# Block-sparse attention and a gated feed-forward layer on one core: scores issued a position ahead of their exponentials, and the gathered values shared between GpSimd and SyncE

## The chip, the cores and the metric

The kernel runs on one core of a Trainium2 chip. The time is that of one execution on the device, in microseconds. Its engines are TensorE (PE, with its weight loads as PEld), VectorE (DVE), ScalarE (ACT), GpSimd (POOL) and SyncE (SP), which here only starts transfers. Each runs its own instruction stream in order; they wait for one another by semaphores.

## The reference

```python
B, H, S, D = q.shape                    # 4, 8, 768, 64; blocks of 32, so 24 blocks
mask = np.abs(blk_i - blk_j) <= 1       # a window of three blocks,
mask |= (blk_i == 0) | (blk_j == 0) | (blk_i == 23) | (blk_j == 23)   # first and last block global,
for qb in range(24):
    for kb in sampled_blocks[qb]:       # and three sampled blocks for each query block
        mask[qb*32:(qb+1)*32, kb*32:(kb+1)*32] = True
attn = softmax(where(mask, q @ k.T / sqrt(D), -1e9))
x = (attn @ v).transpose(0, 2, 1, 3).reshape(3072, 512)
xn = x / sqrt(mean(x*x) + 1e-6) * rms_g
out = (silu(xn @ w_gate) * (xn @ w_val)) @ w_out    # 512 -> 1536 -> 512
```

The sampled blocks are input data: which keys and values a query block needs is known only when the kernel runs.

## The kernel before

Batch 0 is computed densely, in groups of 256 queries; this takes about the first 72 us, and the other batches' keys and queries are loaded and turned beside it. Batches 1 to 3 are computed sparsely, in 18 **chunks** of four query blocks, six chunks to a batch. Five are ordinary (four consecutive blocks); the sixth, the wide one, holds blocks 0, 23, 1 and 22. Blocks 0 and 23 attend to every key, so a wide chunk has eight score bursts instead of four.

For a query block, keys and values lie in 128 rows: slots for the first and the last block, the three window blocks, the three sampled ones, each stored as 16 pairs of rows. Keys are collected in `kg` by copies: the window by DVE (`gather_k`, L471), the sampled blocks by ACT and GpSimd (`sampled_k`, L485), queries by DVE (`gather_q`, L500). Values are collected in `vg` from a table in device memory (`vtab`, L446) by one indirect gather of GpSimd for each query block (`gather_v`, L512), four for an ordinary chunk, two for a wide one, 66 in all. `vg` has two buffers in use; a third is laid over what the dense phase needs.

**Sequence of a chunk.** The loop over the chunks (L1078) runs 19 times, and each turn has ten positions. Jobs are registered for a position by `do(n, f)`. In turn i:

- position 0: the values of chunk i−1 in two halves (`values`, L644, 64 or more small matmuls each), TensorE turns of some chunks, and GpSimd's key copies for the next chunk
- positions 1 and 2: `normalise` of the two halves on DVE (reciprocal L669, multiplication L670)
- positions 1 to 4 (wide: 1 to 8): `scores(i, part)`: eight 64-column matmuls into one PSUM bank (L620), and directly behind them their exponential on ACT (L628), into `ex`, which has three buffers
- position 2: the gathers for the next chunk's values
- positions 3, 4 and 6: DVE's copies of queries and keys for the next chunk; ACT's key copies are spread up to position 9
- position 4: squares on ACT (L677); position 5: `rms_power` on GpSimd (L681, L682); position 7: `x_scaled` on DVE (L698), with a DMA transpose on SyncE (L700) into `xg`, or for four chunks later by TensorE (L707).

Behind every position, `position()` (L798) takes pieces of the feed-forward layer from a list, at a rate that is worked out when a group of chunks enters (groups of 2, 3, 4, 4, 3 and 2 chunks; a group enters at position 4 of the second turn after its last chunk). A **piece** is a gate (L737, then `th` on ACT at L741), a value (L748; `u` at L752 and `hps` at L756 on DVE) or a down projection (L766, then `yo` on ACT at L771 and a store by SyncE at L717 or L726). So TensorE's stream is attention with feed-forward pieces between, in an order that the program fixes; after the last chunk (254 us) only the last group's feed-forward is left.

**PSUM.** Every burst, half of the values, gate, value and down piece takes the next of eight banks in a ring (`bank()`, L103). The next user of a bank waits until the reader of the old content is done.

Of the kernel before, what the change touches and what calls it, by code (L numbers as in the profile page):

```python
# [18 lines left out]
def kernel(  # L19
# [12 lines left out]
    nc = tc.nc  # L32
# [70 lines left out]
    def bank(shape, dtype, name):  # L103
        space, tag = ring[turn_of[0] % len(ring)]
        turn_of[0] += 1
        return space.tile(shape, dtype, name=name, tag=tag)
# [27 lines left out]
    def load_v(b, pr):  # L134
        t = vraw[(b, pr)] = ld.tile([P, 2, NC, D], FP32, name="vraw", tag="vraw", bufs=4)
        if b:
            nc.vector.memset(t[0:1, 0, 0, 0:1], 0.0)
        (nc.sync if b else nc.gpsimd).dma_start(
            out=t, in_=v[b, 2 * pr:2 * pr + 2].rearrange("e (p c) d -> p e c d", p=P))
# [213 lines left out]
    qb_i = const.tile([NS, NB], I32, name="qb_i")  # L353
    vidx = const.tile([P, NB], I32, name="vidx")
    kofs = const.tile([1, NB * NRND], I32, name="kofs")
    qb = const.tile([NS, NB], FP32, name="qb")
    rs = const.tile([NS, NB, NRND], FP32, name="rs")
    pp_i = const.tile([NS, 1], I32, name="pp_i")
# [25 lines left out]
    def index_steps():  # L384
# [24 lines left out]
        for r, lo, hi in ((1, 0, 2 * HB), (0, 0, HB), (2, 2 * HB, 3 * HB)):  # L409
            yield lambda r=r, lo=lo, hi=hi: nc.vector.tensor_scalar(  # L410
                out=vidx[lo:hi], in0=tmp[lo:hi, :, r], scalar1=float(HB), scalar2=pp[lo:hi],
                op0=ALU.mult, op1=ALU.add)


    kat = {}
    ET = mybir.EngineType
# [4 lines left out]
    def address(c, r, n=1):  # L421
        eng = ET.Activation if by_act(c, r) else ET.Pool
        _, vals = nc.values_load_multi_w_load_instructions(
            kofs[0:1, r * NB + c:r * NB + c + n], engines=[eng], min_val=0, max_val=NT - HB,
            skip_runtime_bounds_check_because="a sampled block is one of the sequence's")
        for m, x in enumerate(vals):
            kat[(c + m, r)] = x

    by_need = [(x, r) for i in range(PB) for x in chunks[i][1] if x not in (0, NB - 1)
               for r in range(NRND) if by_act(x, r)]  # L430
# [74 lines left out]
                            in_=spaced(rows[:, :, qbs[lo] * HB:(qbs[lo] + 1) * HB],  # L505
                                       (qbs[lo + 1] - qbs[lo]) * HB, hi - lo, HB))

    def gather_v(i, js=range(QB)):
        b, qbs = chunks[i]
        for j in js:  # L510
            if qbs[j] not in (0, NB - 1):
                nc.gpsimd.indirect_dma_start(  # L512
                    vgs[i % 2][:, j, :], None, vtab[b][:],
                    bass.IndirectOffsetOnAxis(ap=vidx[:, qbs[j]:qbs[j] + 1], axis=0))


    def ex_tile():
# [86 lines left out]

    exs = {}

    def bursts(i):
        return 8 if chunks[i][1][0] == 0 else 4

    def scores(i, part):  # L610
        b, qbs = chunks[i]
        wide = qbs[0] == 0
        heads = H // bursts(i)
        st = bank([P, 512], FP32, "st")
        at = 0
        for h in range(part * heads, (part + 1) * heads):
            of = [(KT[b % 2][:, h, cc::HC], j) for cc in range(HC) for j in range(2)] if wide else []
            of += [(kgs[i % 2][:, h, j, :], j) for j in range(2 if wide else 0, QB)]
            for lhsT, j in of:
                nc.tensor.matmul(  # L620
                    out=st[:, at:at + UN], lhsT=lhsT,
                    rhs=Qd[i % 2][:, h, :, :, j * HB:(j + 1) * HB].rearrange("p a w s -> p (a w) s"),
                    start=True, stop=True)
                at += UN
        if part % 4 == 0:
            exs[(i, part // 4)] = work.tile([P, 4 * 512], BF16, name="ex", tag="ex", bufs=3)
        ex = exs[(i, part // 4)][:, part % 4 * 512:(part % 4 + 1) * 512]
        nc.scalar.activation(  # L628
            out=ex.rearrange("p (u s w) -> p u s w", s=HB, w=2),
            in_=st.rearrange("p (u w s) -> p u s w", s=HB, w=2), func=AF.Exp, scale=SCALE)  # L630

    ops, stages, ssqs, rstds = {}, {}, {}, {}

    def values(i, g):
        b, qbs = chunks[i]
        wide = qbs[0] == 0
        op = bank([P, 512], FP32, "op")
        ops.setdefault(i, []).append(op)
        vg = vgs[i % 2].rearrange("p j (w h x) -> p j w h x", w=2, h=H)
        per = H // bursts(i)  # L640

        def mm(h, j, lhsT, rhs, n, of):
            at = (h % 4) * VW
            nc.tensor.matmul(out=op[j * BLK:(j + 1) * BLK, at:at + VW], lhsT=lhsT, rhs=rhs,  # L644
                             start=(n == 0), stop=(n == of - 1))

        for h in range(4 * g, 4 * g + 4):
            part = h // per
            ex = exs[(i, part // 4)][:, part % 4 * 512:(part % 4 + 1) * 512].rearrange(
                "p (h u w s) -> p h u w s", h=per, w=2, s=BLK)[:, h % per]  # L650
            if not wide:
                for w in range(2):
                    for j in range(QB):
                        mm(h, j, ex[:, j, w, :], vg[:, j, w, h, :], w, 2)
                continue
            for n in range(NC):
                cc, w = divmod(n, 2)
                for j in range(2):
                    mm(h, j, ex[:, 2 * cc + j, w, :], Vs[b % 2][:, 2 * cc + w, h, :], n, NC)
                if n < 2:  # L660
                    for j in range(2, QB):
                        mm(h, j, ex[:, 4 + j, n, :], vg[:, j, n, h, :], n, 2)

    def normalise(i, g):
        if g == 0:
# [184 lines left out]
    def side_work(gi, h):  # L850
# [23 lines left out]
        if gi == 2:  # L874
            if h == 0:
                nc.vector.memset(Vs[1][:, :, :, D:VW], 1.0)
                for b in range(1, B):
                    zero_rows(b)
            if h == 1:
                load_kq(1, 3)  # L880
            if h in (2, 3):
                cast_v(1, 2 * h - 4, pool)
                cast_v(1, 2 * h - 3, pool)
            if h == 3:
                table(1)
                nc.vector.tensor_scalar(out=gain, in0=gain, scalar1=float(DM) ** 0.5,
                                        scalar2=None, op0=ALU.mult)
                nc.vector.memset(eps, DM * 1e-6)
            if h in (3, 4):
                load_kq(2, h - 3)  # L890
            if h > 3:
                load_v(2, h - 4)
            if h == 5:
                gather_v(0)
                for x in sampled_k(0, "pool"):
                    x()
                first_keys.extend(sampled_k(0, "act"))
                first_copies.extend(gather_k(0, dve))
            if h == 7:
                gather_v(1, (0, 1))  # L900
                load_kq(2, 2)

    first_keys, first_copies = [], []
# [174 lines left out]
    for i in range(NCH + 1):  # L1078
        jobs = {}

        def do(n, f):
            jobs.setdefault(n, []).append(f)
# [4 lines left out]
        if i == 0:  # L1087
# [5 lines left out]
            do(6, lambda: enter_dense(cur, distance(0, 6)))  # L1093
            do(4, lambda: nc.vector.memset(Qd[1], 0.0))
            do(3, lambda: load_kq(2, 3))
            do(7, lambda: gather_v(1, (2, 3)))
        else:
            do(0, lambda: values(i - 1, 0))
            do(0, lambda: values(i - 1, 1))
# [7 lines left out]
            if i - 2 in by_pe:  # L1107
                do(0, lambda: x_turned(i - 2))
        if i < NCH:
            n = bursts(i)  # L1110
            for part in range(n):
                do(1 + part, lambda part=part: scores(i, part))
        if b + 1 < B and s <= NP:
            if s < NP:
                do(9 if s == 0 else 0, lambda: cast_v(b + 1, s, act))
# [7 lines left out]
        if nx is not None:  # L1123
# [17 lines left out]
            for m, x in enumerate(kact):  # L1141
                do(at + (m + 1) * (NPOS - 1 - at) // len(kact), x)

            if nx > 1:
                do(2, lambda: gather_v(nx))
        for m in range(min(6, len(by_need)) if i < 2 else 0):
            do(m, next_address)

# [48 lines left out]
```

## The time and the profile before

| | |
|---|---|
| median of three runs | 290.3 us (289.85 to 290.57) |
| the profiled execution | 290.28 us, of it span 288.5 us |
| GpSimd: gathers L512 | 66, mean 992 ns, 65.5 us |
| ACT: exponentials L628 | 84, mean 600 ns, 50.4 us |
| TensorE: gate, value and down pieces L737, L748, L766 | 80.2, 80.0 and 69.1 us |
| DVE: `u` L752 and `hps` L756 | 54.5 and 55.1 us |
| DMA traffic | 47.44 MB, of it 32.60 MB on GpSimd's queue and 14.18 MB on SyncE's |
| start of the values calls, us | 81.5, 90.25, 100.2, 108.8, 115.8, 126.4, 136.1, 145.0, 153.5, 162.3, 172.0, 183.2, 194.3, 202.5, 213.7, 226.7, 239.0, 253.9 |

Times in the profile are microseconds from the start of the span. "Idle before" an instruction is the time its engine stood still ahead of it, and an arrow names what ended it. A row of a stage lists for each engine its busy time in that stretch. A matmul's record covers its way through the array, so records of matmuls that follow one another overlap; what a row of them costs is read from start to start.

### The profile page before, as it was taken

The page shows a single profiled execution, that of the slowest core. Times are in us where ns is not written, and L with a number is a line of the kernel's source. Part 1 is how long each engine was busy: PE and PEld are TensorE (multiplying, and loading weights), DVE is VectorE, ACT ScalarE, POOL GpSimd, SP SyncE. Part 2 cuts the span into 40 slices and gives each one's busy share as a digit, 9 for nine tenths or more (in the row PEclk, how much of TensorE's full clock was granted, in tenths as well). Part 3 has the DMA queues.
Part 4 walks back from the last instruction along what each step waited for, and adds up shares of the span by engine and source line. Part 5 has one row for each costly group of instructions (what it writes and reads, how often), then busy time and mean ns, then how long its engine had stood idle before and what let it go on. Part 6 is the DMA issues. An engine that isn't in the chain of part 4 may idle for free.

```text
span 288.5 us, 9875 instructions
## 1 busy us (share of the span) xinstructions
PE 273.9 (95%) x3840; PEld 185.3 (64%) x3871; DVE 216.7 (75%) x596; ACT 198.2 (69%) x467; POOL 146.7 (51%) x244
## 2 busy tenths in 40 slices
PE   8798999898999899799999999999999999999995
PEld 6586896687668678666665555545545556664783
DVE  7888889678979959966999578796499951784580
ACT  4896786588589789759989878577746484533331
POOL 8857244558487585787887627627723330101000
PEclk9999999999999999999999999999999999999999
DMA  7999999999885479898995845426932252000102
GB/s 133 287 214 201 206 207 268 290 229 315 168 232 125 142 205 287 173 222 259 250 170 154 280 122 154 101 73 186 204 115 77 59 168 77 36 2 36 75 1 73
DMA packets 37426, 47.44 MB, mean 164 GB/s; under 512 B 11184, under 2 KB 29380, under 8 KB 37380
## 3 DMA queue, kind: packets, MB, share of 16 engines
q0 software_dynamic: 21184, 32.60, 51.1%
q1 hardware_dynamic: 16132, 14.18, 17.2%
q8 instruction: 30, 0.49, 0.7%
q14 instruction: 16, 0.13, 0.1%
q10 hardware_dynamic: 64, 0.03, 0.0%
HBM read 46.45 MB, written 8.83 MB: 192 GB/s over the span
## 4 chain that ended last, share of the span: by engine, by line
PE 64%; DVE 16%; DMA 11%; issue 3%; POOL 3%; ACT 2%; DVEq 0%; ACTq 0%; POOLq 0%
PE yp L766 19%; PE gp L737 16%; PE vp L748 15%; PE st L620 5%; DMA gain<-in_moe_rms_g_dram 5%; DVE u L752 4%; DVE hps L756 4%; DMA qbf<-in_q_dram 4%; PE op L644 4%; DMA vraw<-in_v_dram 3%; PE tqk L455 2%; PE st L527 2%; DVE stage L670 1%; DVE xs L698 1%; PE op L536 1%
## 5 line engine op out<-in xcount | busy, mean ns | idle before, releaser
L512 POOL DMA_INDIRECT vg<-vtab,vidx x66 | 65.5, 992 | 45.2 <-PE op L644 27.1
L737 PE MATMUL gp<-xg,wg 128*128 128x256 bf16 (+2 forms) x426 | 80.2, 307 | 2.2 <-DVE stage L670 0.9
L748 PE MATMUL vp<-xg,wv 128*128 128x256 bf16 (+2 forms) x428 | 80.0, 307 | 1.4 <-DVE u L752 0.6
L741 ACT ACTIVATE th<-gp 128x256 bf16<-128x256 f32 (+2 forms) x108 | 49.8, 463 | 37.6 <-PE gp L737 34.4
L752 DVE SCALAR_TENSOR_TENSOR u<-th,gp 128x256 bf16<-128x256 bf16 (+2 forms) x108 | 54.5, 504 | 22.1 <-ACT th L741 21.5
L766 PE MATMUL yp<-wo,hps 128*128 128x512 bf16 (+1 forms) x282 | 69.1, 370 | 1.6 <-issue 0.3
L756 DVE TENSOR_TENSOR hps<-u,vp 128x256 bf16<-128x256 bf16 (+2 forms) x108 | 55.1, 510 | 11.6 <-PE vp L748 0.5
L628 ACT ACTIVATE ex<-st 128x512 bf16<-128x512 f32 x84 | 50.4, 600 | 13.8 <-PE st L620 12.6
L737 PEld LDWEIGHTS <-wg 128*128 128x128 bf16 x432 | 39.7, 98 | 20.0 <-issue 2.0
L748 PEld LDWEIGHTS <-wv 128*128 128x128 bf16 x432 | 39.5, 98 | 18.6 <-issue 1.5
L766 PEld LDWEIGHTS <-hps 128*128 128x128 bf16 x300 | 26.1, 98 | 20.8 <-DMA wo<-in_moe_w_out_dram 0.3
L530 ACT ACTIVATE ex<-st 128x768 bf16<-128x768 f32 x42 | 33.3, 813 | 5.8 <-PE st L527 5.6
L771 ACT ACTIVATE yo<-yp 128x512 f32<-128x512 f32 (+1 forms) x25 | 14.6, 582 | 19.7 <-PE yp L766 19.5
L681 POOL TENSOR_TENSOR ssq<-ssq,eps 128x1 f32<-128x1 f32 x18 | 4.3, 241 | 39.6 <-ACT junk L677 38.1
L527 PE MATMUL st<-wide_q,wide_k 88*128 88x256 bf16 x144 | 22.9, 272 | 1.5 <-DVE wide_q L345 1.1
L644 PEld LDWEIGHTS <-ex 128*32 128x32 bf16 x1344 | 13.6, 95 | 7.8 <-issue 7.8
L670 DVE TENSOR_TENSOR stage<-op,rz 128x256 bf16<-128x256 f32 x36 | 15.3, 425 | 1.2
L644 PE MATMUL op<-vg,ex 128*32 128x66 bf16 x1056 | 15.2, 195 | 1.0 <-DVE u L752 1.0
L527 PEld LDWEIGHTS <-wide_k 88*128 88x128 bf16 x144 | 13.0, 97 | 5.0 <-DVE wide_q L345 2.0
L620 PEld LDWEIGHTS <-kg 128*128 128x128 bf16 x272 | 12.7, 98 | 5.2 <-issue 0.3
L620 PEld LDWEIGHTS <-wide_q 128*128 128x128 bf16 x256 | 12.5, 98 | 5.3 <-issue 0.2
L620 PE MATMUL st<-wide_q 128*128 128x64 bf16 x256 | 15.1, 193 | 0.1
(147 smaller groups left out, 379.6 us busy)
## 6 DMA issues: line engine op xcount, KB each, us to landing
out_dram<-yo SPq DMA_DIRECT2D x20, 256.0 KB
vraw<-in_v_dram SPq DMA_DIRECT2D x12, 384.0 KB
kbf<-in_k_dram POOLq DMA_DIRECT2D x15, 192.0 KB, 5.7
vtab<-Vs POOLq DMA_DIRECT2D x3, 792.0 KB, 6.2
qbf<-in_q_dram POOLq DMA_DIRECT2D x12, 192.0 KB, 8.4
vraw<-in_v_dram POOLq DMA_DIRECT2D x4, 384.0 KB, 6.4
wg<-in_moe_w_gate_dram POOLq DMA_DIRECT2D x4, 384.0 KB, 10.6
wv<-in_moe_w_val_dram POOLq DMA_DIRECT2D x4, 384.0 KB
```

Of the source, the lines that this page charges most:

```text
L512: nc.gpsimd.indirect_dma_start(vgs[i % 2][:, j, :], None, vtab[b][:], bass.IndirectOffsetOnAxis(ap=vidx[:, qbs[j]:qbs[j] + 1], axis=0))
L527: nc.tensor.matmul(out=at[:, e], lhsT=KT0[0:KR, h, jt * P:(jt + 1) * P], rhs=QT0[0:KR, h, c0 * P:(c0 + 2) * P], start=True, stop=True)
L530: nc.scalar.activation(out=ex[:, 3 * part:3 * (part + 1), :], in_=at[:, 0:3], func=AF.Exp, scale=SCALE)
L620: nc.tensor.matmul(out=st[:, at:at + UN], lhsT=lhsT, rhs=Qd[i % 2][:, h, :, :, j * HB:(j + 1) * HB].rearrange("p a w s -> p (a w) s"), sta ...
L628: nc.scalar.activation(out=ex.rearrange("p (u s w) -> p u s w", s=HB, w=2), in_=st.rearrange("p (u w s) -> p u s w", s=HB, w=2), func=AF.E ...
L644: nc.tensor.matmul(out=op[j * BLK:(j + 1) * BLK, at:at + VW], lhsT=lhsT, rhs=rhs, start=(n == 0), stop=(n == of - 1))
L737: nc.tensor.matmul(out=gp[:, 0:tg], lhsT=wg[:, c, f * P:(f + 1) * P], rhs=xg[:, c, 0:tg], start=(c == 0), stop=(c == KD - 1))
L741: nc.scalar.activation(out=th[:, 0:tg], in_=gp[:, 0:tg], func=AF.Tanh, scale=0.5)
L748: nc.tensor.matmul(out=vp[:, 0:tg], lhsT=wv[:, c, f * P:(f + 1) * P], rhs=xg[:, c, 0:tg], start=(c == 0), stop=(c == KD - 1))
L752: nc.vector.scalar_tensor_tensor(out=u[:, 0:tg], in0=th[:, 0:tg], scalar=1.0, in1=gp[:, 0:tg], op0=ALU.add, op1=ALU.mult)
L756: nc.vector.tensor_tensor(out=hps[f][:, 0:tg], in0=u[:, 0:tg], in1=vp[:, 0:tg], op=ALU.mult)
L766: nc.tensor.matmul(out=yp, lhsT=hps[f][:, tt * P:(tt + 1) * P], rhs=wo[:, f, lo:hi], start=(f == 0), stop=(f == NF - 1))
```

## The change

- `scores` is split: the matmuls of part p of an ordinary chunk are issued at position p, the exponential stays at position 1 + p, as a function of its own (`exponentials`). For a wide chunk the eight bursts stand at positions 0, 1, 1, 2, 3, 3, 4, 5 and the exponentials at 1 to 8. In turn 0 all of them are a position later.
- In a wide chunk the matmuls for blocks 0 and 23, which have the same keys, are merged into one of 128 columns.
- Values: for an ordinary chunk blocks 0 and 1 are still gathered by GpSimd, and blocks 2 and 3 come by SyncE's transfers (`fetch_v`): one for the windows of both blocks, one for each sampled block, whose row is a register's value, and broadcasts of the first and last block, which are left out where the buffer still has them. Of a wide chunk, GpSimd gathers one block and SyncE fetches one.
- GpSimd's gathers are now for the chunk after the next, two positions behind an exponential (`behind` copies one element of `ex`, so the queue of GpSimd waits for it). SyncE's transfers, also for the chunk after the next, are at position 8.
- Three buffers of `vg` are used in turn.
- The three indices of a block are packed into one number by DVE and loaded into SyncE's registers in the dense phase (`table_blocks`).

```diff
+    def table_row(c, r):
+        at = nc.s_assert_within((vat[c] >> (5 * r)) & 31, 0, NB, ...)
+        return at * HB
...
-    def gather_v(i, js=range(QB)):
+    def gather_v(i, js):
...
-                    vgs[i % 2][:, j, :], None, vtab[b][:],
+                    vgs[i % 3][:, j, :], None, vtab[b][:],
...
+    def by_pool(i):
+        return (2,) if wide(i) else (0, 1)
+
+    def fetch_v(i):
+        b, qbs = chunks[i]
+        vg, t = vgs[i % 3], vtab[b]
+        j0 = by_pool(i)[-1] + 1
+        n = QB - j0
+        for to, at, none in ((F0, 0, 1), (L0, NT - HB, NB - 2)):
+            if none in qbs[j0:]:
+                at = NT
+            elif i % PB > 2:
+                continue
+            src = t[at:at + HB, :]
+            nc.sync.dma_start(
+                out=vg[to:to + HB, j0:QB, :], in_=src.unsqueeze(1).to_broadcast([HB, n, 2 * HV]))
+        w = t[(qbs[j0] - 1) * HB:(qbs[j0] + 2) * HB, :]
+        step = (qbs[j0 + 1] - qbs[j0]) * HB if n > 1 else 0
+        nc.sync.dma_start(
+            out=vg[W0:W0 + 3 * HB, j0:QB, :],
+            in_=_dc.replace(w.unsqueeze(1), ap=[w.ap[0], [step * 2 * HV, n], w.ap[1]]))
+        for j in range(j0, QB):
+            for r in range(NRND):
+                nc.sync.dma_start(out=vg[R0 + r * HB:R0 + (r + 1) * HB, j, :],
+                                  in_=vtab[b][bass.ds(table_row(qbs[j], r), HB), :])
+
+    def behind(i, part):
+        nc.gpsimd.tensor_copy(out=gate, in_=exs[(i, part // 4)][0:1, part % 4 * 512:part % 4 * 512 + 1])
...
+            if wide(i):
+                for cc in range(HC):
+                    nc.tensor.matmul(
+                        out=st[:, 2 * cc * UN:2 * (cc + 1) * UN], lhsT=KT[b % 2][:, h, cc::HC],
+                        rhs=q[:, :, 0:2 * HB], start=True, stop=True)
...
         if i < NCH:
-            n = bursts(i)
-            for part in range(n):
-                do(1 + part, lambda part=part: scores(i, part))
+            at = [0, 1, 1, 2, 3, 3, 4, 5] if wide(i) else [0, 1, 2, 3]
+            for part, n in enumerate(at):
+                do(n + (i == 0), lambda part=part: scores(i, part))
+            for part in range(bursts(i)):
+                do(1 + part + (i == 0), lambda part=part: exponentials(i, part))
...
-            if nx > 1:
-                do(2, lambda: gather_v(nx))
+            if nx + 1 < NCH:
+                part = 2 if wide(i) else 1
+                do(2 + part + (i == 0), lambda: behind(i, part))
+                do(2 + part + (i == 0), lambda: gather_v(nx + 1, by_pool(nx + 1)))
+                do(8, lambda: fetch_v(nx + 1))
```

## The prediction

> **What bounds the kernel now.** I read the shares and slices first, then the stages, the waits, and the time line around each values call. Durations come from the profiled execution: 290.28 us, 288.5 us of them span and 1.78 us around it. It lies 0.02 us under the median of the runs shown (290.3), so I take its differences as they are.
>
> ```profile
> PE 273.9 (95%) x3840; PEld 185.3 (64%) x3871; DVE 216.7 (75%) x596; ACT 198.2 (69%) x467; POOL 146.7 (51%) x244
> PE   8798999898999899799999999999999999999995
> PEclk9999999999999999999999999999999999999999
> PE 64%; DVE 16%; DMA 11%; issue 3%; POOL 3%; ACT 2%; DVEq 0%; ACTq 0%; POOLq 0%
> L512 POOL DMA_INDIRECT vg<-vtab,vidx x66 | 65.5, 992 | 45.2 <-PE op L644 27.1
> L628 ACT ACTIVATE ex<-st 128x512 bf16<-128x512 f32 x84 | 50.4, 600 | 13.8 <-PE st L620 12.6
> ```
>
> TensorE is busy 95% of the span at full granted clock. GpSimd, whose gathers the change halves, has 3% of the chain; the exponentials' 12.6 us of waiting for scores is idle time of ACT, which has 2%. By stage:
>
> ```profile
> 116.00:126.00 10.00, 8.28 (x166) 6.21 (x156) 9.14 (x27) 7.99 (x24) 7.91 (x14) 1.00 0.84 202
> 172.00:183.00 11.00, 10.84 (x166) 6.30 (x168) 10.02 (x23) 9.24 (x25) 6.57 (x11) 1.00 0.41 112
> 183.00:194.00 11.00, 10.85 (x197) 6.22 (x198) 9.05 (x21) 6.72 (x20) 5.42 (x10) 1.00 0.44 114
> 239.00:254.00 15.00, 14.84 (x239) 9.36 (x243) 7.74 (x18) 7.29 (x15) 0.73 (x2) 1.00 0.13 39
> ```
>
> The columns are the stretch, its length, then PE, PEld, DVE, ACT, POOL busy, clock, DMA share. After 160 us TensorE lacks 0.15 us in 11: any wait that it gains there is paid whole. Before 160 us it lacks more, and what it waits for is mostly DVE: DVE has no idle time over 150 ns in 83.0–104.0, 107.2–126.7 and 134.4–159.8. TensorE's real stalls, summed over 72–160 us, are 6.6 us. The three largest:
>
> ```profile
> 85.98 0.61 PE L737 MATMUL gp<-xg,wg 128*128 128x256 bf16 x4 [0.54 <-DVE stage L670]
> 94.64 0.60 PE L737 MATMUL gp<-xg,wg 128*128 128x256 bf16 x4 [0.69 <-ACT ex L628]
> 117.25 0.43 PE L644 MATMUL op<-vg,ex 128*32 128x66 bf16 x32 [0.99 <-DVE u L752]
> ```
>
> Each is a wait for a PSUM bank: the ring hands out eight banks in order of use, and the next user waits for the reader of the old content.
>
> **The change part by part.**
>
> *Gathers halved (66 to 33), the rest by SyncE.* Takes 33 × 0.992 = 32.7 us from GpSimd, which is not on the path: gathers land 3.4–8.2 us after issue, and values use them 8 us or more later. What it gives the path is DVE: copies L500 take 362 ns where a gather runs beside them (26 of 60), 287 otherwise, so 26 × 75 ns = 2.0 us; half of that is 1.0 us, of which 0.4–0.5 us lies in the saturated stretches. Bounds 0 to −1.0 us; I take −0.4.
>
> SyncE gets 138 more transfers. Nearest rows for issuing: output stores 0.33–0.45 us each, forms with a broadcast 0.5–1.0. An ordinary chunk: six sampled blocks at 0.43 plus an estimated 0.25 for their register work, and one to three wide forms at 0.6, some 4.7–6 us. With the 2.5 us that SyncE issues per chunk today, this fits chunks of 7.0–15 us. The fetch stands at position 8, behind the same chunk's transpose (position 7), and its values come 2.2 chunks later, 15 us or more. It costs nothing while no transpose is queued behind a late fetch; the transposes with least slack (issued 100.35 and 201.85, used 105.01 and 206.83, landed after 3.3 and 3.9) have 1.0–1.5 us. Without that cover each costs up to a fetch, 5 us. Bounds 0 to +5; taken 0.
>
> The Trainium skill, "DMA: Bandwidth & Descriptors", section "Rules for kernel authors", speaks against this part: transfers under 64 KB should be coalesced, and spreading them over issuing engines saves only issue time. The sampled pieces here are 33 KB; no row of this profile prices such a piece, and the rows above agree that what is saved is issue time on an engine off the path. By that rule this part gives 0 and the sum below is 1.85, by the rows it gives −0.4 and the sum is 1.45.
>
> *Waits in the values.* In the order of the built programs the values of a chunk now wait for up to nine SyncE transfers in place of one queue; TensorE gets 48 more semaphore instructions. In the trace such an instruction takes 51 ns, two in a row come 125 ns apart, but its sequencer runs them ahead of the array (one ran at 103.95 for a matmul at 105.01). Bounds: 0 if all are run ahead, 48 × 0.125 = 6.0 us if none. Nearest to the first, since they follow long matmuls: +0.2.
>
> *The gates (16 one-element GpSimd copies) and the tables.* A gather now waits for an exponential, and `rms_power` and key copies are queued behind it. GpSimd's slack to `xs` is about 0.9 us at 116.7 and near 0 at 169.2, where the new gathers also wait for their table (landed 113.3 and 166.0). Bounds −0.3 to +0.5; taken 0, as the gate's two exponentials are done early. Six register loads and four small DVE operations in the dense phase: under 0.3 us, taken 0.
>
> *Wide chunks' scores merged.* 72 pairs of 64-column matmuls (29 ns start to start) become 72 of 128 columns (56): 72 × 2 ns = −0.15 us.
>
> *Scores a position ahead.* ACT's order stays. So no exponential's queue changes, and its 12.6 us of idle time shrinks off the path. TensorE has three effects:
>
> (a) The first burst comes directly behind the values instead of behind a feed-forward piece, so its keys are needed earlier. ACT's last sampled-key copy ends, after the start of the values, at 1.19 (chunk 1), 1.07 (chunk 4), 0.92 (chunk 7) and 0.7 or less elsewhere; values end near 0.64. New stall 0.55, 0.43 and 0.3. Chunks 1 and 7 are in stretches where DVE is late anyway. At chunk 4 it isn't (`hps` at 110.12 waits for `vp`, ended 110.06): +0.4 (bounds 0.3–0.65).
>
> (b) With bursts ahead, the ring comes round sooner to the bank that the values' second half wrote. From the programs' order, columns of matmul between that write and the bank's next use fall from 9728 to 8192 for the values run at the start of chunks 11 and 12, from 14848 to 10240 at 16 (and at chunk 2, where DVE is the bound). The bank is free when `normalise(1)` ends:
>
> ```profile
> 172.62 1.04 PE L737 MATMUL gp<-xg,wg 128*128 128x512 bf16 x3
> 175.93 0.42 DVE L670 TENSOR_TENSOR stage<-op,rz 128x256 bf16<-128x256 f32 x1
> ...
> 185.11 1.04 PE L737 MATMUL gp<-xg,wg 128*128 128x512 bf16 x3
> 188.42 0.42 DVE L670 TENSOR_TENSOR stage<-op,rz 128x256 bf16<-128x256 f32 x1
> ```
>
> In the new order, with 0.21 us for a burst (in the trace of before `st` at 185.98 to `vp` at 186.21; I take a little less) and 0.86 for a piece of four 512-column matmuls, TensorE reaches the bank at 11 at 172.62 + 0.21 + 0.86 + 2 × 0.21 + 0.86 + 0.21 + 0.86 = 176.04. The stage ends at 176.35 or, if DVE's `hps` ahead of it comes one burst later, at 176.55: +0.3 to +0.5. At 12: 185.11 + 4 × 0.21 + 3 × 0.86 = 188.53, against 188.84–189.04: +0.3 to +0.5. At 16 by the same working: 231.59 against 231.90–232.10, +0.3 to +0.5. All three lie where TensorE lacks nothing, so no other wait absorbs them; sum +0.9 to +1.5, taken +1.4, near the upper end, since whatever delays TensorE's pieces delays DVE's `hps` ahead of the stage too.
>
> (c) Stalls that can go: the 0.7 us at 94.64 (a gate takes the bank of the burst just written) is gone in the new order. What is late next there is DVE, without idle time until 104.0, so nothing of it is kept: 0, at best −0.7.
>
> **Sum:** −0.4 + 0.2 + 0 − 0.15 + 0.4 + 1.4 = +1.45, so 290.28 + 1.45 = **291.7 us**.
>
> **The rivals.**
>
> *Nothing net.* DVE finishes `normalise(1)` earlier by the fewer gathers, the bank waits stay under 0.2 us each and the key copy is absorbed: +1.45 − 1.4 − 0.4 + 0.6 = +0.25. For it: the waits come out of differences of 0.3 us. Against: DVE runs no L500 copy ahead of those stages at 11 and 12. 290.5 (289.4–291.2).
>
> *Faster, on the other side.* TensorE's waits and DVE's backlog before 160 us feed each other: ACT's `th` is queued behind exponentials that wait for scores, DVE's `u` waits for `th`:
>
> ```profile
> ACT ex L628 <- PE st L620: 12.6, 15, 2.7
> DVE u L752 <- ACT th L741: 21.5, 15, 5.5
> PE op L644 <- DVE u L752: 1.0, 1, 1.0
> ```
>
> If scores that are ready early let `th` and `u` run earlier, DVE's 1.0 us of copies and a third of the 6.6 us of stalls (2.2) go: −3.2 + 1.45 = −1.75, 288.5 us. It decides if DVE's idle times at 104.0 (3.2 us, behind `th`) and 126.7 (2.1) shrink. Against: those wait for gates that wait for `xg`, not for scores.
>
> *SyncE's queue or the added waits bind.* A fetch ahead of a transpose, 1–5 us late at one or two group entries, or a third of the 48 semaphores unhidden (2.0 us): 291.7 + 2 to + 4 = 293.7–295.7. For it: SyncE waits 68.8 us for `yo`, and what is queued behind waits too:
>
> ```profile
> SPq L726 <- ACT yo L771: 68.8, 13, 18.9
> ```
>
> Against: values two chunks away, DMA share 0.13–0.68 after 160 us.
>
> *It does not do what it says.* The order of the programs shows bursts a position ahead, 33 gathers and 198 SyncE copies; only the freeing of ACT can fail, if the exponentials were not late in a place that matters, which is the forecast itself.
>
> The Trainium skill, same page, section "Issuing engines are not separate DMA queues", says that transfers from SyncE and GpSimd interleave on the same 16 DMA engines. No run here separates this yet; with the DMA share at 0.8–1.0 in 104–160 us it would leave landing times as they are, so the sum does not change by it and the faster rival gets no more.
>
> **Chances.** Forecast 0.40 (291.2–292.7), nothing net 0.22, faster 0.22, SyncE or semaphores 0.16. A measurement of this kernel tells apart 0.3%, 0.87 us. Faster than 289.4: 0.22; within 289.4–291.2: 0.23 (the first rival, and as much of the forecast's low edge as that rival loses to faster); slower: 0.55. The range goes from 288.6, a little over the centre of the faster rival, to 294.5, inside the last one: some 0.1 is left out on each side.
>
> **What would show it.** Right: gathers 33 on GpSimd with 33 us less busy time; L628 idle for `st` well under 12.6; TensorE waits of 0.3–0.6 us for DVE `stage` L670 near the pieces three positions into chunks 11, 12 and 16; a wait of a burst for ACT's L485 copy at chunk 4; DVE busy 1 us less. Wrong: TensorE idle in the values behind SyncE's transfers or before `gp` for a late transpose (the last rival); DVE's `u` starting earlier in 83–160 us and TensorE's stalls there under 5 us (the faster one); no new wait after 160 us (nothing net).

## The result, and the profile after

The changed kernel takes 298.98 us (median of 4 runs, 297.84 to 300.30), the kernel before on the same chip 290.08: a ratio of 1.031 (95% interval 1.0261 to 1.0358). Forecast was 291.7 us in a range of 288.6 to 294.5, so the sign was right and the size was not: 8.9 us were lost, not 1.45. Ratios and their intervals, here and below, go by the fast runs of a kernel alone, so they can differ from the quotient of the medians, which are over all its runs. The profiled execution of the changed kernel took 300.30 us, 298.5 of them span.

The first lines of its page, to be set against those of before, with the gathers and the exponentials:

```profile
PE 277.8 (93%) x3770; PEld 187.9 (63%) x3799; DVE 216.1 (72%) x599; ACT 197.7 (66%) x467; POOL 117.4 (39%) x227
PEclk9999999999999999998999999999999999999999
PE 60%; DVE 25%; issue 5%; ACT 3%; DMA 3%; POOL 1%; ACTq 0%; DVEq 0%; POOLq 0%
L538 POOL DMA_INDIRECT vg<-vtab,vidx x33 | 33.5, 1015 | 17.4 <-issue 4.1
L705 ACT ACTIVATE ex<-st 128x512 bf16<-128x512 f32 x84 | 50.1, 601 | 11.6 <-PE st L695 10.6
```

The change does what it says: 33 gathers, 32 us less of them. But DVE's share of the chain went from 16 to 25%, "issue" from 3 to 5%, and in one slice TensorE's clock is not full.

Where the time went is read from the starts of the values calls (the first matmul of each call in line 644, here 720) and from the end of the span:

| values call | before | changed | later by | in this step |
|---|---|---|---|---|
| 1 | 81.52 | 81.63 | 0.11 | |
| 6 (the first wide chunk) | 126.45 | 129.50 | 3.05 | 2.94 |
| 7 | 136.08 | 142.84 | 6.76 | 3.71 |
| 11 | 171.99 | 179.16 | 7.17 | 0.41 |
| 13 | 194.35 | 202.23 | 7.88 | 0.71 |
| 15 | 213.67 | 223.13 | 9.46 | 1.58 |
| 17 | 239.00 | 249.09 | 10.09 | 0.63 |
| end | 288.51 | 298.53 | 10.02 | −0.07 |

TensorE's waits with the names of their releasers, from the time line of the changed kernel (start, length, operation, idle time before it):

```profile
83.05 0.71 PE L695 MATMUL st<-wide_q 128*128 128x64 bf16 x8 [0.71 <-DVE wide_q L525]
96.02 0.41 PE L695 MATMUL st<-Qd,kg 128*128 128x64 bf16 x8 [0.79 <-DVE stage L747]
111.72 0.31 PE L695 MATMUL st<-Qd,kg 128*128 128x64 bf16 x5 [0.53 <-ACT kg L510]
122.68 0.61 PE L825 MATMUL vp<-xg,wv 128*128 128x256 bf16 x4 [0.36 <-DVE stage L747]
...
133.37 0.29 PE L720 MATMUL op<-Vs,ex 128*32 128x66 bf16 x4 [2.31 <-issue]
...
183.87 0.35 PE L683 MATMUL st<-wide_q,wide_k 128*128 128x128 bf16 x3 [0.35 <-DVE stage L747]
196.51 1.04 PE L825 MATMUL vp<-xg,wv 128*128 128x512 bf16 x4 [0.33 <-DVE stage L747]
216.12 1.04 PE L814 MATMUL gp<-xg,wg 128*128 128x512 bf16 x4 [0.94 <-DMA xg<-xs]
241.84 0.33 PE L683 MATMUL st<-Qd,KT 128*128 128x128 bf16 x3 [0.53 <-DVE stage L747]
```

Three causes can be told apart in these rows.

**Waits for a bank, a key or a query** (`stage`, `kg`, `wide_q`). Those at 111.7, 183.9, 196.5 and 241.8 us are the four that the prediction named and priced. The one at 96.0, at chunk 2, it named and took for free. The one at 83.0, ahead of chunk 1's first burst, it had not. The one at 122.7 is no loss, since the kernel before has it too:

```profile
120.72 0.61 PE L737 MATMUL gp<-xg,wg 128*128 128x256 bf16 x4 [0.35 <-DVE stage L670]
```

**One stop without a releaser, 2.31 us long (2.5 from start to start), near the end of the first wide chunk's values.** "Issue" means that nothing the profile shows was waited for. Instructions come by transfers too: the page's DMA part has a queue "q8 instruction" of 30 packets with 0.49 MB, so 16 KB each, and TensorE runs some 7700 instructions, 256 to a packet. One of these packets started at 130.60 us, was done at 131.89, and TensorE went on at 133.37. Counting TensorE's instructions from the start (two for each weight load, which has a matmul behind it, since some records of matmuls are missing, and one for each semaphore instruction), the stop falls where the count is 194 over a multiple of 256. The other stops without releaser over 0.6 us that the runs below show on this kind of chip have a remainder of 193 or 194 too. TensorE had come past the cut before (remainder 194) 10 instructions ahead of these values, and a wide chunk's values are 256 instructions that take 1.5 us: the block was used up before the next was there.

The windows of the changed kernel show what the stop leaves behind (the columns are the stretch, its length, the engines, the clock, the DMA share):

```profile
129.00:134.00 5.00, 2.69 (x136) 2.07 (x134) 0.00 (x0) 0.60 (x2) 1.25 (x5) 0.93 1.16 274
134.00:138.00 4.00, 3.78 (x36) 2.27 (x36) 3.34 (x10) 2.05 (x5) 0.81 (x2) 0.66 0.69 116
```

The clock was 0.5 from 133.3 to 136.7 us. So 2.5 us of standing still cost 3.7. The Trainium skill, "TensorE: Matmul & The Clock Gate", section "Why this matters for your kernels", warns of idle gaps over about 3 us; here 2.5 us were enough, and 1.1 us (second set below) were not.

**A transpose that comes late.** The gate at 216.12 us waits 0.94 us for `xg`. SyncE's time line of the changed kernel:

```profile
203.92 0.98 SPq L558 DMA_DIRECT2D vg<-vtab  x2
204.96 0.42 SPq L562 DMA_DIRECT2D vg<-vtab  x1
205.64 4.14 SPq L567 DMA_DIRECT2D vg<-vtab  x6
209.88 3.67 SPq L803 DMA_DIRECT2D out_dram<-yo  x5
213.64 1.23 SPq L777 DMA_TRANSPOSE xg<-xs  x1
```

One fetch keeps SyncE 5.9 us, the output stores queue up behind it, and the transpose behind these; it landed 2.43 us after its issue, just ahead of the gate.

### The profile page after: what moved, and what is told of

Its sections match the earlier page's. It is cut to its first block, busy times and chain, and to the rows that moved or that the text cites. A ratio compares the mean times of both kernels' runs of the same rounds, so it can differ in the third digit from the quotient of the medians.

```text
span 298.5 us, 10274 instructions
## 1 busy us (share of the span) xinstructions
PE 277.8 (93%) x3770; PEld 187.9 (63%) x3799; DVE 216.1 (72%) x599; ACT 197.7 (66%) x467; POOL 117.4 (39%) x227
## 4 chain that ended last, share of the span: by engine, by line
PE 60%; DVE 25%; issue 5%; ACT 3%; DMA 3%; POOL 1%; ACTq 0%; DVEq 0%; POOLq 0%
PE yp L843 16%; PE gp L814 13%; PE vp L825 13%; DVE hps L833 5%; DVE u L829 5%; PE op L720 3%; PE st L586 3%; PE st L695 3%; DMA vtab<-Vs 2%; DVE stage L747 2%; PE op L595 2%; PE tqk L480 2%; DVE junk L629 1%; PE unread L228 1%; DVE xs L775 1%
## 5 line engine op out<-in xcount | busy, mean ns | idle before, releaser
L829 DVE SCALAR_TENSOR_TENSOR u<-th,gp 128x256 bf16<-128x256 bf16 (+2 forms) x108 | 54.4, 504 | 26.1 <-ACT th L818 25.5
L705 ACT ACTIVATE ex<-st 128x512 bf16<-128x512 f32 x84 | 50.1, 601 | 11.6 <-PE st L695 10.6
L814 PEld LDWEIGHTS <-wg 128*128 128x128 bf16 x432 | 40.3, 98 | 21.2 <-DMA xg<-xs 1.4
L843 PEld LDWEIGHTS <-hps 128*128 128x128 bf16 x300 | 26.9, 98 | 22.8 <-issue 1.4
L538 POOL DMA_INDIRECT vg<-vtab,vidx x33 | 33.5, 1015 | 17.4 <-issue 4.1
L573 POOL COPY gate<-ex 1x1 bf16<-1x1 bf16 x16 | 3.0, 188 | 66.8 <-ACT ex L705 62.3
L586 PE MATMUL st<-wide_q,wide_k 88*128 88x256 bf16 x144 | 23.5, 275 | 2.1 <-ACT ex L589 1.0
L758 POOL TENSOR_TENSOR ssq<-ssq,eps 128x1 f32<-128x1 f32 x18 | 3.6, 201 | 40.2 <-ACT junk L754 40.0
L695 PEld LDWEIGHTS <-kg 128*128 128x128 bf16 x256 | 12.0, 100 | 6.1 <-issue 1.5
L695 PE MATMUL st<-Qd,kg 128*128 128x64 bf16 x256 | 13.6, 196 | 1.5 <-DVE stage L747 0.8
```

Source lines behind the costliest of these rows:

```text
L538: nc.gpsimd.indirect_dma_start(vgs[i % 3][:, j, :], None, vtab[b][:], bass.IndirectOffsetOnAxis(ap=vidx[:, qbs[j]:qbs[j] + 1], axis=0))
L586: nc.tensor.matmul(out=at[:, e], lhsT=KT0[0:KR, h, jt * P:(jt + 1) * P], rhs=QT0[0:KR, h, c0 * P:(c0 + 2) * P], start=True, stop=True)
L695: nc.tensor.matmul(out=st[:, at:at + UN], lhsT=kgs[i % 2][:, h, j, :], rhs=q[:, :, j * HB:(j + 1) * HB], start=True, stop=True)
L705: nc.scalar.activation(out=ex.rearrange("p (u s w) -> p u s w", s=n, w=2), in_=st.rearrange("p (u w s) -> p u s w", s=n, w=2), func=AF.Exp ...
L814: nc.tensor.matmul(out=gp[:, 0:tg], lhsT=wg[:, c, f * P:(f + 1) * P], rhs=xg[:, c, 0:tg], start=(c == 0), stop=(c == KD - 1))
L829: nc.vector.scalar_tensor_tensor(out=u[:, 0:tg], in0=th[:, 0:tg], scalar=1.0, in1=gp[:, 0:tg], op0=ALU.add, op1=ALU.mult)
```

## The experiments

The theories: **A**, the loss has three parts, the waits that early scores bring, the stop and the late transpose, and SyncE's transfers cause the last two. **B**, early scores bring nearly all of it. Later **C** (the stop is a matter of where the stream of instructions is cut) and **R** (early scores lose through the ring of PSUM banks) against **K** (they lose through keys that are needed earlier and through missing cover).

### First set, on another chip

The edits. Early scores alone, in the kernel before (the exponentials become a function of their own, as in the change):

```diff
+            at = [0, 1, 1, 2, 3, 3, 4, 5] if chunks[i][1][0] == 0 else [0, 1, 2, 3]
+            for part, n in enumerate(at):
+                do(n + (i == 0), lambda part=part: scores(i, part))
```

> The kernel before, with nothing but the score matmuls a position ahead of their exponentials. Theory A (the loss of 8.9 us has three parts: 3 to 4 us of waits that early scores bring, 3.7 us from a stall of TensorE inside the wide values at 131 us with a slow clock behind it, which SyncE's transfers cause, and some 1.4 us from a transpose that comes late behind SyncE's transfers): 293.0 to 294.5 us, with waits of TensorE for DVE's stage near 176, 188.5 and 232 us. Theory B (early scores bring nearly all of it, SyncE's transfers are hidden): 296 us or more.

The changed kernel with the scores back:

```diff
-                do(n + (i == 0), lambda part=part: scores(i, part))
+                do(1 + part + (i == 0), lambda part=part: scores(i, part))
```

> The changed kernel with the score matmuls put back directly ahead of their exponentials; gathers and SyncE's transfers as changed. Theory A: 290.1 + 3.7 + 1.4, so 294.5 to 296 us, and the stall without a named releaser inside the first wide chunk's values is there. Theory B: 291.5 us or less.

The changed kernel with all gathers on GpSimd (`by_pool` gives all blocks, no `fetch_v`):

> The changed kernel with all 66 gathers on GpSimd again, two chunks ahead in three buffers, and no transfer of values by SyncE. Theory A: as the early scores alone, 293 to 294.5 us; no stall in the first wide chunk's values, no slow clock at 134 us. Theory B: as the changed kernel, 297 to 299 us.

The changed kernel with `by_pool(6)` giving all blocks, and no fetch for chunk 6:

> The changed kernel, but the values of chunk 6 alone (whose SyncE transfers run at 124 to 130 us) are all gathered by GpSimd. TensorE's instructions come by transfers too, 16 KB at a time; one started at 130.6 us, nearly 6 us behind the point that asked for it, and TensorE stood still from 131.0 to 133.4. Theory A (SyncE's transfers of chunk 6 hold that load up): the stall is gone, 295 to 296 us. Rival (it only depends on where the instruction stream is cut into loads, which this does not move): the stall stays, 298 to 299.5 us.

| kernel | us | ratio (interval) |
|---|---|---|
| before, on this chip | 314.62 | |
| early scores alone | 320.37 | 1.0214 (1.0092 to 1.0336) |
| changed, all gathers on GpSimd | 318.10 | 1.0120 (1.0026 to 1.0214) |
| changed, scores back | 296.76 | 0.9450 (0.9359 to 0.9541) |
| changed, chunk 6 by GpSimd | 301.43 | 0.9598 (0.9493 to 0.9703) |

No theory had expected this: on this chip the kernel before takes 24 us more than on the prediction's, and the kernels with half of the gathers do not. The time line of early scores alone, with all 66 gathers, shows how it loses:

```profile
86.55 0.95 POOL L512 DMA_INDIRECT vg<-vtab,vidx  x1 [0.30 <-issue]
87.81 0.95 POOL L512 DMA_INDIRECT vg<-vtab,vidx  x1 [0.30 <-issue]
89.06 0.95 POOL L512 DMA_INDIRECT vg<-vtab,vidx  x1 [0.30 <-issue]
89.62 0.42 DVE L761 TENSOR_TENSOR hps<-u,vp 128x256 bf16<-128x256 bf16 x1 [2.07 <-PE vp L753]
91.17 0.38 ACT L746 ACTIVATE th<-gp 128x256 bf16<-128x256 f32 x1 [2.21 <-remote]
```

DVE and ACT wait 2 us for matmuls that were done: the gate's matmuls that ACT waits for ended at 88.0 us. TensorE's signals were recorded at 86.67, 88.16, 89.60 and 91.09 us, one every 1.5 us, and then seven of them within 0.35. If the recorded signals are matched in order to the instructions that give them, some 110 of TensorE's in this run are over 0.3 us late, and for some 95 of these a gather runs in the meantime; stretches of the same lengths at random would meet a gather in 58% of the cases. In the kernel before on the prediction's chip there are 4 such signals, all beside a gather. So on this chip late signals go with gathers, and the kernels with 66 of them take 315 to 320 us, those with 33 to 35 take 297 to 301. Why is not settled, and no run separates a gather from its other traffic. Times of this chip are not used further, but they show where halved gathers are worth something. The run with all gathers on GpSimd, which was to show whether the stop needs SyncE's transfers, decides nothing: with the late signals its clock too was at 0.5, from 129.8 to 136.6 us.

The stop in the first wide chunk's values was there with chunk 6 by GpSimd too, 0.72 us of "issue" at the same cut. The packet started 0.1 us after the values instead of 1.1; with scores back, on the same chip, the stop was 2.32 us. So both count: where the cut lies, and how late the packet is. (The "nearly 6 us" in what was expected counts from a point that no row shows; from where the array had come to the cut before, the changed kernel's packet started 2.3 us late.)

### Second set, on a chip like the prediction's (before: 289.98 us)

> The changed kernel as it is, beside the others on this chip. On the chip of the first experiments the kernel before took 314.6 us and not 290, and signals between engines came late there while GpSimd was in a gather. On a chip like the prediction's: 298 to 300 us, with the stall of TensorE 1.4 us into the first wide chunk's values. On a chip like that of the first experiments: 298 to 303 us, faster than the kernel before, since it has half of the gathers.

> The changed kernel with 32 more matmuls (64 more TensorE instructions) in the same time at the very start, where TensorE only keeps itself awake (44 of 64 columns instead of 12 of 256). Nothing else moves but the place at which TensorE's instruction stream is cut into loads of 256. Theory C (the stall at 131 us is there because a cut falls 10 instructions ahead of the wide values, whose 256 instructions are done in 1.5 us, sooner than the next load comes): the cut moves 64 instructions ahead, the stall and the slow clock behind it are gone, 295 to 296 us on a chip like the prediction's. Theory A (SyncE's transfers hold the load up, wherever the cut is): no change, 298 to 300 us.

```diff
-    keep_busy(12, 256, unread)
+    keep_busy(44, 64, unread)
```

> Scores a position ahead in the kernel before, again, beside the changed kernel. On a chip like the prediction's, theory A: 293.0 to 294.5 us; theory B (early scores bring nearly all of the loss): 296 us or more. On a chip like that of the first experiments: some 320 us.

> The changed kernel with the scores put back directly ahead of their exponentials, again. On a chip like the prediction's: 294.5 to 296 us by theory A, with the stall in the first wide chunk's values (its stream is cut at the same place); 291.5 us or less by theory B. On a chip like that of the first experiments: some 297 us.

| kernel | us (lowest to highest) | ratio (interval) |
|---|---|---|
| changed | 296.66 (295.88 to 298.01) | 1.0244 (1.0217 to 1.0271) |
| changed, cut moved by 64 | 296.19 (294.28 to 297.27) | 1.0191 (1.0143 to 1.0240) |
| early scores alone | 294.73 (294.24 to 295.12) | 1.0161 (1.0144 to 1.0178) |
| changed, scores back | 293.36 (290.86 to 296.75) | 1.0085 (1.0049 to 1.0120) |

None of the four medians lies in a range that had been expected: the changed kernel is 1.3 us under its range, the one with the cut moved 0.2 over C's, early scores 0.2 over A's, and scores back between A's and B's. Theory B falls even so: early scores cost 4.7 us, sharing the values 2.5 by the ratio, and both together 6.7 here. By the profiles, the changed kernel is faster than on the day of the prediction mostly because its stop was shorter: here 1.1 us, with the clock at 1.00 behind it. The cut is at the same place, so the length of the stop differs by how late the packet is. Scores back had it 3.8 us long in its profile, which is its slowest run; its runs lie as far apart as 290.86 and 296.75.

With the cut moved the stop is gone from the wide values. The window of the wide turn in the changed kernel:

```profile
128.60:139.00 10.40, 9.39 (x200) 6.16 (x200) 4.88 (x14) 6.64 (x19) 5.41 (x12) 1.00 0.96 220
```

The same turn with the cut moved:

```profile
130.30:139.60 9.30, 9.25 (x200) 6.08 (x200) 4.88 (x14) 6.62 (x19) 5.45 (x12) 1.00 0.93 227
```

The same 200 matmuls' records, 1.0 us less of TensorE standing still; the turn takes 9.3 us, in the kernel before 9.6. The median moved by only 0.5 us, less than expected: this kernel loses 1.2 us ahead of the first values call (82.32 against 81.08), which may be the edit's own, and 0.8 us at 162.8, again at a cut, where a packet came 5.7 us after the cut before. By its median this run decides nothing; by its places it speaks for C, with A's slow packets as the second condition.

That packets come later with SyncE's fetches can be read from all profiles on chips of this kind. Between 80 and 170 us they start on average 1.4 to 2.2 us after TensorE's array has come to their cut in the seven profiles with fetches, and 0.6 to 0.9 us in the six without. Six of the seven have a stop at a cut of 0.7 us or more, none of the six has. The kernels with fetches also have half of the gathers, and no run on these chips separates the two.

### Third set (before: 290.38 us)

Normalise of the second half a position earlier, on early scores alone:

```diff
-            do(2, lambda: normalise(i - 1, 1))
+            do(1, lambda: normalise(i - 1, 1))
```

> Scores a position ahead in the kernel before (294.7 us), and DVE's normalise of the second half at position 1 instead of 2, directly behind the first half's. Theory R (early scores bring the ring of PSUM banks round before DVE has read the values' second half; waits for that multiplication are 0.96 us at 95, 0.51 at 122, 0.33 at 142, 0.49 at 180, 0.49 at 192 and 0.47 at 236 us, 3.2 us in all): most of these go, 292.0 to 293.0 us. Rival K (the loss is the missing cover behind the values: keys needed earlier, weight loads not hidden): 294.2 to 295.5 us.

Early scores for the ordinary chunks only (wide chunks `at = [1, 2, 3, 4, 5, 6, 7, 8]`):

> Scores a position ahead in the kernel before, but only for the ordinary chunks; the wide chunks' bursts stand at their exponentials again. By the starts of the values calls the wide turns 5, 11 and 16 took 1.07, 0.52 and 0.47 us longer with early scores. Theory R: 292.5 to 293.2 us, that is 2.1 less than with all of them early. Rival (what a wide turn seems to lose would be lost in the next turn anyway, since DVE is behind): 294 us or more.

Scores back, and the cut moved at a place where TensorE has time:

```diff
-                keep_busy(1, 512)
+                keep_busy(12, 64)
```

> The changed kernel with the scores put back, and with 33 more small matmuls (66 TensorE instructions) at about 22 us, where TensorE waits for ACT anyway (three times 12 of 64 columns for one of 512), so that the cut of the instruction stream falls 66 instructions ahead of the first wide chunk's values. Theory C (the late load only hurts where 256 instructions are used up sooner than it comes): no stall there, clock 1.000, 290.0 to 291.5 us, with what is left a transpose that comes 1 us late at 213 us. Theory A (SyncE's transfers delay the loads, another cut is hit instead): 292.5 us or more, with a stall of a few tenths to 2 us without a releaser in another place.

> The changed kernel with both changes: the cut moved by 66 instructions, and normalise of the second half at position 1. Theory R and C together: 296.7 less 1.1 to 3.7 less some 2, so 292 to 293.5 us. If neither holds: 296 us or more.

| kernel | us (lowest to highest) | ratio (interval) |
|---|---|---|
| early scores, normalise early | 292.46 (291.81 to 292.75) | 1.0066 (1.0051 to 1.0081) |
| early scores, wide chunks back | 292.93 (292.65 to 293.23) | 1.0089 (1.0075 to 1.0103) |
| scores back, cut moved | 290.04 (288.67 to 292.47) | 0.9999 (0.9974 to 1.0025) |
| changed, both mended | 292.08 (291.21 to 292.61) | 1.0058 (1.0041 to 1.0075) |

All four medians lie in the ranges of R and C. The third run shows a sign of A too: it has stops at two other cuts, 0.91 us at 114.8 and 0.72 us at 159.0, and the late transpose that was expected to be left is not there. Of the waits of early scores alone

```profile
95.45 0.41 PE L622 MATMUL st<-Qd,kg 128*128 128x64 bf16 x8 [0.79 <-DVE stage L675]
111.10 0.30 PE L622 MATMUL st<-Qd,kg 128*128 128x64 bf16 x5 [0.54 <-ACT kg L485]
121.91 0.61 PE L753 MATMUL vp<-xg,wv 128*128 128x256 bf16 x4 [0.35 <-DVE stage L675]
```

the ones for `stage` at 95, 180, 192 and 236 us are gone with an early normalise, and 2.3 us with them, while those at 121 and 142 us stay. Turn 2 shows it best: 0.74 us longer than before with early scores, 0.07 with the early normalise as well. (This kernel has a late transpose of its own, 0.83 us ahead of a gate at 106.3, without any fetch by SyncE.) With the cut moved, sharing the values costs nothing in sum (0.9999), and the clock is 0.998 to 1.000 in all twelve runs. The window of the wide turn of that kernel:

```profile
127.00:136.30 9.30, 9.25 (x204) 6.09 (x205) 5.35 (x16) 6.58 (x19) 5.65 (x12) 1.00 1.08 251
```

### Fourth set: the controls (before: 290.31 us)

> Scores a position ahead in the kernel before and normalise of the second half at position 1 (292.5 us), with the first burst of each chunk back at position 1, behind a feed-forward piece. If the rest of the loss is the first burst's (keys and queries needed earlier, waits of 0.5 us at 83, 0.5 at 91 and 0.7 at 110 us): 291.0 to 291.8 us. If it is in the ring or in the wide turn at 117 to 126 us: 292.2 us or more.

> The kernel before with normalise of the second half at position 1 and nothing else. If that edit mends the waits that early scores bring and little besides: 289.7 to 290.6 us, as the kernel before. If it is a gain of its own (the kernel before too waits 0.5 us for that multiplication at 86 us), so that the ring explains less: 288.0 to 289.0 us.

> The changed kernel with the scores put back and the cut of TensorE's stream moved (290.0 us), and normalise of the second half at position 1. By the ring theory there is little for that edit to mend without early scores: 289.5 to 290.5 us. If it is a gain of its own: 288 to 289 us, a version that beats both kernels.

All three have the edit of normalise shown above; the first has `at = [1, 1, 2, 3]`, wide `[1, 1, 1, 2, 3, 3, 4, 5]` as well.

| kernel | us (lowest to highest) | ratio (interval) |
|---|---|---|
| early scores, normalise early, first burst back | 291.52 (290.58 to 293.01) | 1.0041 (1.0025 to 1.0056) |
| before, normalise early | 290.04 (289.47 to 290.22) | 0.9990 (0.9981 to 1.0000) |
| scores back, cut moved, normalise early | 288.70 (288.00 to 289.80) | 0.9940 (0.9924 to 0.9956) |

In the kernel before, normalise early gives 0.3 us; with early scores it gave 2.3. So it mends what early scores do to the ring, as R has it. The first burst accounts for 0.9 us of the 2.1 that were left. Of the remaining 1.2, 1.0 us is in the wide turn 5 by the starts of the values calls, and with the wide chunks' bursts back at their exponentials that turn lost nothing; which of its early bursts brings the loss, and by what wait, is not shown. The last kernel beats both: 288.70 us, 0.6% under the kernel before, by the shared values, the merged wide scores, three buffers and normalise early, and without early scores. Its gain of 1.3 us over the one without normalise early lies in the range of the rival, not in that of the ring theory, which had 289.5 us or more. In the one profile of each, some 0.9 us of it is a stop at a cut (at 159.0 us) that this kernel does not have; whether that holds for their other runs is not shown.

## Why the prediction was wrong, point by point

By the starts of the values calls, the 10.0 us by which the changed kernel's profile is longer are made up so: 3.7 us in the turn of the stop (turn 6), 4.5 that early scores alone lose too in the second set, 1.2 at the late transpose (turn 14), 0.5 in turn 1, and 0.1 elsewhere. The sum had 1.8 for early scores and no term for the stop; the late transpose and GpSimd's new order were taken as 0. The step that failed with the largest loss in one place is thus "Waits in the values": it priced semaphores and took TensorE's stream of instructions for always at hand. The next is (b) before 160 us, at chunk 2 and in the wide turn 5.

- **What bounds the kernel.** Right after 160 us. Wrong before it: "before 160 us it lacks more, and what it waits for is mostly DVE" was used as if a new wait of TensorE there were free. What failed in (b) is "and at chunk 2, where DVE is the bound", which gave that wait no price. As (c) has it, the 0.69 us ahead of a gate at 94.64 went, but a wait of 0.79 at 95.45 came in its place, ahead of the chunk's fourth burst, for DVE's second normalise; turn 2 took 0.74 us longer in early scores alone, and normalise early gave nearly all of it back. The wide turn 5, which was not worked out at all, took 1.07 longer; normalise early gave back 0.4 of that, and the rest stays open. A reading of this, not tested by itself: an engine that is late by TensorE's waits is not a cover for further ones, as DVE's next `u` and `hps` wait for gates and values that come later.
- **(b) at chunks 11, 12 and 16.** Forecast 0.3 to 0.5 us each, 1.4 in all. Measured as waits, from start to start, 0.51, 0.49 and 0.69 us; as time by the turns 0.53, 0.18 and 0.64 (changed against before), 1.35. Right in place and cause, and in the size of the sum; at 12 less than half of its wait reached the time.
- **(a) at chunk 4.** Forecast 0.4, measured 0.38 (turn 4), with the wait for `kg` where it was named. Chunk 1 has such a wait too. In early scores alone it is 0.31 us, and turn 1 takes 0.06 longer, so there it was free as forecast.
- **The gates and tables, −0.3 to +0.5, taken 0.** In the changed kernel chunk 1's first burst waits 0.71 us for DVE, and turn 1 takes 0.56 longer; neither early scores alone nor sharing the values alone has that. One of DVE's key copies for that burst takes 1.65 us there (80.63 to 82.28) in place of 0.29, and so it does in the other profiles with shared values. GpSimd's key copies for the same chunk now come behind the gathers, at 80.66 us, just beside it, and not at 77.86 as before. That the one slows the other is not tested; the cost is at the upper end of the stated bounds.
- **Waits in the values, +0.2.** The 48 semaphore instructions cost nothing that shows. What the term lacked is the instruction stream itself: that edits move the cuts of 256 instructions, and that one of them now lies just ahead of a wide chunk's values, 256 instructions that are used up in 1.5 us. It cost 3.7 us with the slow clock behind it, the largest loss in one place on the day of the prediction, and 0.8 in the second set. No view read before the prediction pointed at it but perhaps the "issue" rows (7.8 us before L644's weight loads), which the prediction does not use; that these have to do with packets is not shown. The Trainium skill, "Runtime: NRT & Kernel Launch", section "Instruction fetch mechanics", says that crossing such a boundary is mostly hidden. In these runs it is in the kernels without SyncE's fetches; with them it was not where 256 instructions last 1.5 us, and in three kernels not at a cut some 5 to 8 us behind the last one either (stops of 0.7 to 0.9 us).
- **SyncE, 0 of 0 to +5.** The rival was right in its mechanism, a transpose behind a late fetch, and in its place; by its wait it took 0.9 us at one group entry (1.2 by the turn) and 0.3 in the second profile of the same kernel, and the four kernels with the cut moved have no such wait. Its length of a fetch (4.7–6 us) was right: 5.9. The 0.25 us of register work for each sampled block stood on no row of before; in the changed kernel most of these pieces come 0.65 us apart, half of it the transfer's issue.
- **Halved gathers, −0.4.** The copies became faster as worked out: the copies of line 500 before add up to 7.0 + 6.3 + 3.8 + 2.5 = 19.6 us, and 17.6 after, 2.0 less. (In the trace of before, copies without a gather beside them take 300 ns, not 287, so the working should have given 1.6.) How much of it reached the end is not settled: sharing the values with the cut moved is 0.9999 of before, with two stops in its profile; with normalise early in both, it is 288.70 against 290.04 us, by all its parts together. So neither price, 0 or −0.4, is shown to be the better one. On the chip of the first set the kernel with shared values and without early scores took 296.8 us and the kernel before 314.6, for a reason that no row of the one profile could show.
- **The faster rival** fell: ACT's wait for scores went from 12.6 to 10.6 us, and DVE's wait for `th` rose from 21.5 to 25.5.

## What to carry to other kernels

Moving producers ahead of their consumers also moves them ahead of everything else in a ring of buffers: work out the ring for every turn, and price a new wait of the main engine in full unless a run shows that it is free. A sum of instructions says nothing of where the instruction stream is cut; when a kernel changes by a few per cent, look for stops without a releaser at a fixed remainder, and move the cut before judging the edit. And compare on more than one chip: the same kernel differed by 24 us between chips here, and on one of them halving the gathers gained 18 us that it did not gain on the others.

## What the runs showed of the hardware

- TensorE's instructions come in packets of 16 KB (30 of them, 0.49 MB). On chips like the prediction's, a packet of the sparse part of this kernel starts between 3 us before TensorE's array is at a cut and 5.7 us after it and takes 0.9 to 2.5 us. Where TensorE had run dry it went on 1.2 to 1.6 us after the packet's end, in each of nine stops.
- With SyncE's fetches, packets between 80 and 170 us started 1.4 to 2.2 us after the array was at their cut on average, without them 0.6 to 0.9.
- A stop of 2.5 us brought the clock to 0.5 for 3.4 us; one of 1.1 us did not. On the first set's chip, four stops of 0.5 to 1.2 us between 118.5 and 122 us were followed by the slow clock too.
- On one of the chips, TensorE's signals to other engines came late, one of them 3 us behind the end of its matmuls, mostly beside GpSimd's gathers, and the same kernel took 314.6 us there and 290 elsewhere.
